# Agent attention with a mixture of experts: the second batch's expert is asked for twelve half steps later in SyncE's order

## The chip, the core and the metric

The kernel runs on one core of a Trainium2 chip. The metric is the device time of one execution in microseconds (us). Engines are named as in the profile: PE is TensorE's matmuls, PEld its weight loads, DVE is VectorE, ACT is ScalarE, POOL is GpSimd and SP is SyncE, which here does no arithmetic but asks for nearly all DMA transfers.

## The reference

Two stages follow each other. Agent attention works on q, k and v of shape [4, 11456, 128] with 49 agents per batch. Its result, 45,824 rows of 128, goes through a mixture of 8 experts with one expert per row.

```python
a2k = softmax(scale * agents @ k^T)        # 49 x 11456, per batch
agent_v = a2k @ v                          # 49 x 128
x = softmax(scale * q @ agents^T) @ agent_v
logits = (x / |x|) @ (emb / |emb|)^T / tau
e = argmax(logits); gate = softmax(logits)[e]
out = gate * (relu(x @ w1[e]) @ w2[e])     # w1: 128 x 1024, w2: 1024 x 128
```

## The kernel before, in words

**Batches.** The four batches are worked through one after another. A batch's rows lie in 23 tiles t (four columns of 128 rows each, the last one smaller), and in 12 units u of two tiles for everything that is loaded. For a batch the kernel first reads all k (scores against the agents, with a running maximum) and all v (`k2_unit`, whose product `avp` is added up in `avx`), folds them in `av_chain` into the agents' values, and then guesses in `pick_expert` the one expert `e0i` that the rows of the batch will want. Rows that turn out to want another expert, or to need more hidden units than were kept, are answered at the end.

**The expert's chain.** `pick_expert` computes `e0i` on PE and DVE (L638 to L647), calls `load_expert`, and then prepares the expert: `total` over the squares of `w1s` (L688 on ACT, L252 on PE), `first_layer` (`gp`, L682), a ranking of the 1024 hidden units by strength (L712 to L755, much of it on DVE), the kept units' matrices `gh` and `gl` (L769, L771), the linear remainder `lin` (L797), the second layer's `w2p` (L810) and `vm` (L832). A tile of the batch starts with `hp` (L1168, L1169), which needs `gh` and `gl`, and goes on with `yp` (L1192 to L1206), which needs `lin` and `w2p`.

**SyncE's queue.** `load_expert` reads the expert's number into a register of SP (L837, which waits for DVE's `e0i`), and then asks for the two matrices `w1s` and `w2s` (L840, L841, 512 KB each). SP works in order, and in the order in which the program was written (`manual_schedule`): loads of k, v and q (`unit_load`, L161) and the transposes through the DMA (`kT`, L481, which needs `ks`; `tt`, L894, which needs POOL's `e`) stand behind whatever stands ahead. The units' tiles `kt`, `vt` and `qt` share one ring of ten buffers (LB), so a load waits until the tile asked for ten loads earlier has been read.

**The order of the program.** Every part is a Python generator. A loop over 92 ticks per batch (23 tiles times 4) runs all of them forward by two half steps a tick, counted in `now`; a `yield n` in `pick_expert` of a batch after the first means "go on n half steps later", since it is spawned with half=True. The order of PE, DVE, ACT and POOL is then made by a planner, which takes a time line of its own and the order of the program as priority. SP keeps the program's order.

**The place of the change in that order.** The counter follows from the program alone. In the kernel before it stands at 220 when the second batch's `load_expert` is reached. The requests on SP that follow are: q unit 11 of the first batch and `kT` of k unit 2 of the third batch at 224, k unit 4 of the third at 226, q unit 0 of the second and `tt` of q unit 9 of the first at 228, k unit 5 of the third at 230 and q unit 1 of the second at 232. The first batch's tile 16 begins its `hp` at 227. `w2p` of the second batch is written at 268, its first tile begins `hp` at 285 and `yp` at 295. The third batch's `load_expert` stands at 394, its `w2p` at 442, its first `yp` at 479.

Of the kernel before, what the change touches and what calls it, by code (L numbers as in the profile page):

```python
# [29 lines left out]
def kernel(ctx: ExitStack, tc: tile.TileContext, q, k, v, agents, emb, tau, w1, w2, out):  # L30
# [517 lines left out]
    def av_chain(b, g):  # L548
# [18 lines left out]
        if b == 0:  # L567
            bt.pick = pick_expert(b, 0)
            next(bt.pick)
        else:  # L570
            spawn(pick_expert(b, 1), 1, half=True)
# [56 lines left out]
    def pick_expert(b, g):  # L628
# [18 lines left out]
        dve.tensor_scalar(e0i, e0i, E - 1, None, ALU.bitwise_and)  # L647
        NM, FV = NMS[b], FVS[b]
        FM = NM * P
        w1s, w2s = load_expert(e0i)  # L650
        bt.e0i = e0i
        bt.e0 = sm.tile([P, 1], F32, name="e0", tag="e0")
# [4 lines left out]
        NX = max(NMS)  # L657
        gh = wk.tile([P, NX * P], F16, name="gh", tag="gh")[:, :FM]
        gl = wk.tile([P, NX * P], F16, name="gl", tag="gl")[:, :FM]
        vm = wk.tile([P, FW], F16, name="vm", tag="vm")[:, :FV]  # L660
# [12 lines left out]
        def col(nm, dt=F32):  # L673
            return sm.tile([P, NF], dt, name=nm, tag=nm)
# [79 lines left out]
        for c in range(NF):  # L754
            dve.tensor_scalar(sel[:, c, :FM], iotaf[:, :FM], rank[:, c : c + 1], None, ALU.is_equal)  # L755
            if c % 4 == 3:
                yield g

        def placed(h, w):
            t_ = psx("placed")[:, :w]  # L760
            with in_place(y_last):
                for c in range(NF):
                    pe.matmul(out=t_, lhsT=gt16[:, h, c].rearrange("p h a -> p (h a)"), rhs=sel[:, c, :w],
                              start=(c == 0), stop=(c == NF - 1))
            return t_

        gmx = sm.tile([P, 2], F32, name="gmx", tag="gmx")
        yield 2 * g
        act.copy(gh, placed(0, FM))  # L769
        yield g  # L770
        dve.tensor_copy(gl, placed(1, FM))  # L771
        bt.gh, bt.gl = gh, gl
# [4 lines left out]
        mask = col("mask")  # L777
        dve.tensor_scalar(mask, rank, FM + FV - 0.5, BIG, ALU.is_lt, ALU.mult)
        yield 1
# [56 lines left out]
    def load_expert(ei):  # L836
        ev = sp.value_load(ei[:1, :1], min_val=0, max_val=E - 1)  # L837
        w1s = ld.tile([P, F], F32, name="w1s", tag="w1s", bufs=1)
        w2s = ld.tile([P, NF, D], F32, name="w2s", tag="w2s", bufs=1)
        sp.dma_start(out=w1s, in_=w1[bass.ds(ev, 1), :, :].rearrange("o d f -> (o d) f"))  # L840
        sp.dma_start(out=w2s, in_=w2[bass.ds(ev, 1), :, :].rearrange("o (c p) d -> p (o c) d", p=P))  # L841
        return w1s, w2s
# [760 lines left out]
    with tc.manual_schedule(engines={mybir.EngineType.SP}):  # L1603
        due = []
        for i in range(len(ticks) + LAG):
            if i < len(ticks):
                b, t, r = ticks[i]
# [12 lines left out]
            while due and due[0][0] <= i:  # L1620
                _, b, t, f = due.pop(0)
# [55 lines left out]
```

## Time and profile before

| | |
|---|---|
| time, median of 3 runs | 741.65 us (741.39 to 742.32) |
| the profiled execution's own time | 741.78 us |
| its span, first to last instruction | 740.0 us |
| PE busy | 688.6 us, 93% |
| DVE, ACT, POOL busy | 77%, 64%, 46% |
| mean granted clock of PE | 0.972 |
| chain that ended last: PE, DVE, DMA, ACT, issue, POOL | 56, 23, 6, 5, 4, 4% |

Busy time and granted clock are read together: a matmul at half clock counts as busy for about twice as long. A bracket behind a row of a time line gives the idle time just before it on its engine and what ended it.

### The profile page before, as it was taken

What the parts mean: (1) busy time and instruction counts of PE and PEld (TensorE: products, weight loads), DVE (VectorE), ACT (ScalarE), POOL (GpSimd) and SP (SyncE); (2) the same over time, 40 slices, a digit from 0 to 9 for tenths busy, and PEclk for the clock granted to TensorE, in tenths of its full rate; (3) what the DMA queues carried; (4) which work ended last, traced back from release to release, by engine and by line L of the source; (5) the groups of instructions that cost most, each with busy time, mean ns of one, the idle gap of its engine ahead of it and who ended that gap; (6) DMA issues with size and microseconds to landing.
All of it is one profiled execution on the core that took longest, in us unless ns stands there. A gap on an engine that the chain in (4) does not pass through costs nothing.

```text
span 740.0 us, 23507 instructions
## 1 busy us (share of the span) xinstructions
PE 688.6 (93%) x9416; PEld 574.9 (78%) x9416; DVE 568.1 (77%) x1499; ACT 475.6 (64%) x1161; POOL 338.8 (46%) x576
## 2 busy tenths in 40 slices
PE   8997889989978899999999889989999999999996
PEld 6886678867867788788888778878897776787675
DVE  4676887864457999988558998965658899789886
ACT  3436858667457757877758837865669447766772
POOL 5003401572245557655615836565638356255410
PEclk9998999999969999999999999999999999999998
DMA  8986239846389786598659439945452247223211
GB/s 329 278 306 215 94 73 249 187 137 197 95 205 342 154 199 166 148 279 214 160 158 268 112 67 253 287 124 159 135 172 94 81 87 194 62 60 115 61 45 64
DMA packets 157817, 122.59 MB, mean 166 GB/s; under 512 B 78727, under 2 KB 134105, under 8 KB 157707
## 3 DMA queue, kind: packets, MB, share of 16 engines
q1 hardware_dynamic: 144331, 97.44, 51.1%
q10 hardware_dynamic: 13120, 23.47, 9.1%
q8 instruction: 74, 1.21, 0.7%
q14 instruction: 36, 0.29, 0.1%
q0 software_dynamic: 256, 0.17, 0.1%
HBM read 79.14 MB, written 23.72 MB: 139 GB/s over the span
## 4 chain that ended last, share of the span: by engine, by line
PE 56%; DVE 23%; DMA 6%; ACT 5%; issue 4%; POOL 4%; SPq 0%; ACTq 0%; POOLq 0%; DVEq 0%
PE sp L430 8%; PE fTp L417 6%; PE avp L521 6%; PE hp L1168 4%; PE hp L1169 4%; PE yp L1192 3%; PE yp L1201 3%; DVE hh L1178 3%; PE yp L1204 3%; PE yp L1206 3%; PE yp L1205 3%; PE vp L1017 3%; DMA kt<-in_k_dram 2%; DVE ot L1220 2%; DMA xq<-in_q_dram,ix 1%
## 5 line engine op out<-in xcount | busy, mean ns | idle before, releaser
L1026 ACT ACTIVATE vp<-vp 128x512 f32<-128x512 f32 x191 | 112.3, 588 | 31.7 <-PE vp L1014 16.3
L1178 DVE SCALAR_TENSOR_TENSOR hh<-hp,hh 128x512 f16<-128x512 f32 (+1 forms) x147 | 98.4, 675 | 24.5 <-ACT hh L1177 23.9
L1204 PE MATMUL yp<-w2p,hh 128*128 128x128 f16 (+1 forms) x582 | 109.9, 220 | 0.0
L1205 PE MATMUL yp<-w2p,hh 128*128 128x128 f16 (+1 forms) x582 | 109.8, 220 | 0.0
L1206 PE MATMUL yp<-w2p,hh 128*128 128x128 f16 (+1 forms) x582 | 108.5, 220 | 0.0
L1177 ACT ACTIVATE hh<-hp 128x512 f16<-128x512 f32 (+1 forms) x147 | 85.1, 587 | 34.9 <-PE hp L1169 28.7
L430 PEld LDWEIGHTS sp<-aT_all,fT 128*64 128x64 f32 (+1 forms) x2400 | 83.7, 140 | 23.2 <-issue 11.5
L430 PE MATMUL sp<-aT_all,fT 128*64 128x49 f32 (+1 forms) x2400 | 97.6, 228 | 3.8 <-DVE qe L874 1.4
L1168 PE MATMUL hp<-tt,gh 128*128 128x512 f16 (+1 forms) x207 | 77.5, 377 | 4.3 <-DVE fT L420 2.4
L1169 PE MATMUL hp<-tt,gl 128*128 128x512 f16 (+1 forms) x207 | 77.8, 378 | 0.0
L965 POOL TENSOR_TENSOR nrm<-qq,half 128x16 f32<-128x16 f32 (+2 forms) x28 | 70.4, 2515 | 0.3
L884 POOL TENSOR_TENSOR e<-qe,e 128x392 f16<-128x392 f32 (+1 forms) x44 | 38.1, 866 | 68.0 <-ACT e L881 67.8
L1220 DVE TENSOR_TENSOR ot<-yp,gs 128x512 f32<-128x512 f32 (+1 forms) x92 | 61.1, 670 | 9.3 <-PE yp L1206 3.7
L1201 PE MATMUL yp<-w2f,hh 128*128 128x128 f32 (+1 forms) x456 | 66.7, 284 | 0.0
L1192 PE MATMUL yp<-lin,tt 128*128 128x128 f16 x720 | 63.3, 221 | 2.9 <-DVE w2p L810 1.4
L1204 PEld LDWEIGHTS <-hh 128*128 128x128 f16 (+1 forms) x582 | 57.6, 99 | 10.3 <-issue 0.5
L422 ACT COPY fT<-fTp 128x512 f32<-128x512 f32 (+1 forms) x87 | 48.6, 563 | 24.7 <-PE fTp L417 17.9
L1206 PEld LDWEIGHTS <-hh 128*128 128x128 f16 (+1 forms) x582 | 57.5, 99 | 8.1 <-issue 1.5
L1205 PEld LDWEIGHTS <-hh 128*128 128x128 f16 (+1 forms) x582 | 57.4, 99 | 5.8 <-issue 0.3
L1201 PEld LDWEIGHTS yp<-w2f,hh 128*128 128x128 f32 (+1 forms) x456 | 58.9, 194 | 2.9 <-issue 1.1
L926 POOL TENSOR_TENSOR rt<-rt 128x384 f32<-128x384 f32 (+1 forms) x48 | 40.5, 843 | 45.1 <-DVE rt L923 42.0
L417 PE MATMUL fTp<-ident,qt 128*128 128x128 f32 x360 | 57.0, 288 | 3.3 <-ACT fT L422 1.1
(373 smaller groups left out, 1786.3 us busy)
## 6 DMA issues: line engine op xcount, KB each, us to landing
kt<-in_k_dram SPq DMA_DIRECT2D x44, 512.0 KB, 6.6
vt<-in_v_dram SPq DMA_DIRECT2D x44, 512.0 KB, 6.2
qt<-in_q_dram SPq DMA_DIRECT2D x44, 512.0 KB, 5.5
out_dram<-ot ACTq DMA_DIRECT2D x88, 256.0 KB, 3.4
w1s<-in_moe_w_dram SPq DMA_DIRECT2D x8, 512.0 KB, 4.6
w2s<-in_moe_w_dram SPq DMA_DIRECT2D x8, 512.0 KB, 5.6
tt<-e SPq DMA_TRANSPOSE x44, 4.1
kt<-in_k_dram SPq DMA_DIRECT2D x4, 96.0 KB, 5.8
```

Source lines behind the costliest of these rows:

```text
L417: pe.transpose(out=tp[:, c * p : (c + 1) * p], in_=src[:p, c0 + c, :], identity=ident[:p, :p])
L430: pe.matmul(out=s[h : h + w, c * A : (c + 1) * A], lhsT=xT[:, c * p + h : c * p + h + w], rhs=aT_all[:, b, :], start=True, stop=True, skip ...
L1026: act.activation(z[:p], z[:p], AF.Relu, scale=-1.0, accum_out=bt.vsum[:p, at : at + 1])
L1168: pe.matmul(out=hp[:, :m], lhsT=bt.gh[:, fs], rhs=tt, start=True, stop=False)
L1169: pe.matmul(out=hp[:, :m], lhsT=bt.gl[:, fs], rhs=tt, start=False, stop=True)
L1177: h_last[:] = [act.activation(hh[:, :m], hp[:, :m], AF.Relu)]
L1178: dve.scalar_tensor_tensor(out=hl[:, :m], in0=hp[:, :m], scalar=0.0, in1=hh[:, :m], op0=ALU.max, op1=ALU.subtract)
L1192: pe.matmul(out=yp[:p, c, :], lhsT=tc_, rhs=bt.lin[:, h], start=(c == 0 and h == 0), stop=False, skip_group_check=True)
L1201: y_last[:] = [pe.matmul(out=y, lhsT=hh[:, cs], rhs=bt.w2f[:, f], start=False, stop=last, skip_group_check=True)]
L1204: pe.matmul(out=y, lhsT=hh[:, cs], rhs=wh, start=False, stop=False, skip_group_check=True)
L1205: pe.matmul(out=y, lhsT=hh[:, cs], rhs=wl, start=False, stop=False, skip_group_check=True)
L1206: y_last[:] = [pe.matmul(out=y, lhsT=hl[:, cs], rhs=wh, start=False, stop=last, skip_group_check=True)]
```

## The change

One statement is added to `pick_expert`. For the second batch alone (b == 1) the generator pauses for twelve half steps after `e0i` was computed and before `load_expert` is called. The read of the number and the two loads are so written into SP's order twelve half steps later, at 232 instead of 220, and everything that `pick_expert` writes behind them moves by the same twelve. Neither an instruction nor a byte is added or taken away.

```diff
         dve.tensor_scalar(e0i, e0i, E - 1, None, ALU.bitwise_and)
         NM, FV = NMS[b], FVS[b]
         FM = NM * P
+        if b == 1:
+            yield 12
         w1s, w2s = load_expert(e0i)
         bt.e0i = e0i
         bt.e0 = sm.tile([P, 1], F32, name="e0", tag="e0")
```

## Rows read from the trace of the kernel before

**Rows 1.** The page's first part: busy us, share of the span, instructions.
```profile
PE 688.6 (93%) x9416; PEld 574.9 (78%) x9416; DVE 568.1 (77%) x1499; ACT 475.6 (64%) x1161; POOL 338.8 (46%) x576
```

**Rows 2.** Waits of SP's queue, 186 to 240: us in total, times, longest.
```profile
SPq L837 <- DVE e0i L647: 16.4, 1, 16.4
```

**Rows 3.** Time line of SP: start us, us, queue, line, what; 186 to 392.
```profile
189.16 0.38 SPq L161 DMA_DIRECT2D kt<-in_k_dram  x1
206.79 0.36 SPq L840 DMA_DIRECT2D w1s<-in_moe_w_dram  x1
...
207.82 0.52 SPq L161 DMA_DIRECT2D qt<-in_q_dram  x1
208.51 4.07 SPq L481 DMA_TRANSPOSE kT<-ks  x1
...
213.77 1.23 SPq L894 DMA_TRANSPOSE tt<-e  x1
...
215.78 0.52 SPq L161 DMA_DIRECT2D qt<-in_q_dram  x1
...
388.12 0.36 SPq L840 DMA_DIRECT2D w1s<-in_moe_w_dram  x1
```

**Rows 4.** Busy time by stretch: stretch, us, engines' busy us, PEclk, DMA share, GB/s.
```profile
202.00:207.00 5.00, 3.17 (x49) 2.81 (x49) 3.07 (x17) 0.96 (x5) 0.97 (x3) 0.99 0.00 0
209.00:213.00 4.00, 1.29 (x19) 1.04 (x18) 0.94 (x4) 2.47 (x5) 3.50 (x3) 0.83 1.08 277
213.00:224.00 11.00, 10.93 (x56) 9.74 (x57) 6.74 (x23) 7.51 (x14) 1.62 (x6) 0.53 1.13 295
226.00:232.00 6.00, 3.54 (x52) 2.73 (x51) 4.96 (x12) 3.81 (x8) 2.33 (x3) 1.00 1.12 335
```

**Rows 5.** Time line of PE, 204 to 229: four of its rows.
```profile
204.37 0.38 PE L252 MATMUL total<-avsq,ones 128*128 128x1 f32 x2 [1.46 <-ACT lr L574]
...
211.53 0.38 PE L252 MATMUL total<-wsq,ones 128*128 128x1 f32 x2 [1.69 <-ACT sel L688]
212.93 0.30 PE L417 MATMUL fTp<-ident,qt 96*128 96x96 f32 x1 [1.02 <-DMA qt<-in_q_dram]
...
227.70 1.09 PE L417 MATMUL fTp<-ident,qt 128*128 128x128 f32 x8 [1.12 <-ACT fT L422]
```

**Rows 6.** Time line of ACT: two rows that waited for a load.
```profile
210.33 1.06 ACT L688 ACTIVATE sel<-w1s 128x1024 f16<-128x1024 f32 x1 [2.69 <-DMA w1s<-in_moe_w_dram]
...
225.86 1.06 ACT L466 ACTIVATE ks<-kt 128x1024 f16<-128x1024 f32 x1 [1.88 <-DMA kt<-in_k_dram]
```

**Rows 7.** Time lines of DVE, POOL and PE: what the seven requests wait for.
```profile
190.99 1.28 DVE L476 SCALAR_TENSOR_TENSOR ks<-kt,hsc,ks 128x1024 f16<-128x1024 f32 x1 [0.35 <-ACT ks L470]
...
198.64 0.91 POOL L884 TENSOR_TENSOR e<-qe,e 128x392 f16<-128x392 f32 x1 [10.20 <-ACT e L881]
...
196.05 1.07 PE L521 MATMUL avp<-vt,kd 128*64 128x129 f32 x16
199.67 1.32 PE L521 MATMUL avp<-vt,kd 128*64 128x129 f32 x20
...
205.79 0.15 DVE L647 TENSOR_SCALAR e0i<-e0i 128x1 int32<-128x1 int32 x1
```

**Rows 8.** Tile w2p, batches 2 and 3: durations ns min/median/max, first and last start.
```profile
L1204 PE MATMUL yp<-w2p,hh x83: 216/219/220, 281.4 to 343.0; 128*128 128x128 f16 x83
L810 DVE CAST w2p<-w2pp x1: 677/677/677, 269.4 to 269.4; 128x512 f16<-128x512 f32 x1
...
L1204 PE MATMUL yp<-w2p,hh x40: 218/219/220, 441.3 to 469.6; 128*128 128x128 f16 x40
L810 DVE CAST w2p<-w2pp x1: 676/676/676, 440.0 to 440.0; 128x512 f16<-128x512 f32 x1
```

**Rows 9.** Busy time by stretch, as rows 4: the chains' later stages.
```profile
235.00:282.00 47.00, 43.92 (x604) 37.30 (x604) 40.92 (x102) 33.03 (x83) 28.85 (x52) 1.00 0.78 198
360.00:400.00 40.00, 39.99 (x530) 35.93 (x528) 22.86 (x63) 25.77 (x63) 14.72 (x21) 1.00 0.65 188
405.00:435.00 30.00, 24.21 (x240) 19.97 (x239) 28.22 (x86) 21.88 (x51) 20.21 (x36) 0.95 0.41 113
432.00:436.00 4.00, 4.00 (x20) 3.58 (x20) 3.97 (x14) 2.80 (x5) 1.42 (x2) 0.57 0.00 0
```

## The prediction

> **What bounds the kernel now.** I read the page's first part, then the clock and the busy time by stretch, then SP's waits, then the time lines around the longest of them. PE is busy for 93% of the span [rows 1], so whatever leaves it idle or at half clock is on the path, and little else is. The stage of the change is one of the few where this happens. SP's longest wait there is the read of the second batch's number: 16.4 us, from 189.5 (end of the k load) to 206 [rows 2, 3]. Behind it the queue is stopped: from 202 to 207 the DMA moves nothing [rows 4]. Then everything comes at once. `w1s` goes out at 206.79, and its square on ACT waits 2.69 us for it [rows 3, 6]; PE, which works in its planned order, waits for that square 1.69 us and then for the q load that stood behind the matrices 1.02 us [rows 5]. From 209 to 213 PE is busy for 1.29 of 4 us, and from 213 to 224 it is busy but at a granted clock of 0.53, so at 1.2 GHz for most of it [rows 4].
>
> **The change, part by part.** Nothing is added; two things move.
>
> First, SP's order. Seven requests (the loop's counter in the section on the kernel names them) now stand ahead of the read: four loads whose buffers must be free, one `kT`, one `tt`, and a last q load. Before, they took from 207.82 to 216.30, 8.5 us, waits among them included [rows 3] (the first and the last of the seven). Were they ready earlier? `ks` for the `kT` is written at 192.27, `e` for the `tt` at 199.55 [rows 7]. The ring of ten gives the first q load the buffer of the third last unit of v, read until 197.12, and the last q load that of the last unit, read until 200.99 (the two `avp` rows) [rows 7]. So they can start at 197.1 and need 8.5 us: SP reaches the read at about 205.6, while `e0i` is written at 205.94 [rows 7]. The read then waits for almost nothing and `w1s` goes out at the same 206.8. If the `kT` takes longer than its 4.07 us the matrices come later by that much; the bound is the whole 8.5 us, should none of the seven start before the read does today. What lies behind the read on SP is as before, but starts at 207.8 where it started at 216.4: 8.6 us earlier. Below, the cost is nothing.
>
> Second, the chain's order. `total`, `first_layer` and all behind them have their priority twelve half steps later. How long is that? The first `yp` of the second and third batch start at 281.4 and 441.3 [rows 8], so 92 ticks or 184 half steps take 159.9 us: 0.87 us a half step, 10.4 us for twelve. So some 10 us of work of the first batch's tiles, which begin at count 227, go ahead of `total`. They need `tt` of unit 8 (transposed before the long wait) and later that of unit 9, which now comes at about 202. `w1s` lands at about 210.3 as before, or up to 3.5 us later if the new loads share the DMA with it (its whole trip was 206.79 to 210.33) [rows 3, 6]; with 10 us of cover PE doesn't see it. If that cover were missing, the 1.69 us would stay.
>
> The terms on PE:
> - the idle time from 209 to 213: 4.00 − 1.29 = 2.7 us goes [rows 4], since both its releasers, the square of `w1s` and the q load, are no longer last.
> - the half clock from 213 to 224: 10.93 us busy at 0.53 is 10.93 × 0.47 = 5.1 us of lost work [rows 4]. Bounds: 5.1 and nothing; I take it whole, because this fall follows the idle stretch of the first term.
> - 226 to 232: 2.46 us idle [rows 4]. The 1.12 us in it go back to ACT, which stood 1.88 us waiting for a k load from the burst [rows 5, 6]; with k loads 8.6 us earlier I count these 1.1 as gone and leave the rest. Bounds: 0 and 2.5.
>
> Together 8.9 us (0 to 10.3). The 1.46 us of waiting at 204 [rows 5] and the thin stretch around it stay: this is `av_chain` itself, which nothing here moves.
>
> On the clock, the trace shows a fall just behind each of these idle stretches. The Trainium skill (TensorE: Matmul & The Clock Gate, "HAM oscillation — how this bites in real kernels") says that every wait for a transfer between bursts of matmuls can send the clock to half again, each time to be paid anew. By that the second fall belongs to the second wait and the 5.1 us go, as I took it; but it also speaks against the change, since a new wait further on would cost its own fall.
>
> **What is given back.** The chain is long. From the asking for `w1s` to `w2p` it took 269.4 + 0.7 − 206.8 = 63.3 us in the second batch and 440.0 + 0.7 − 388.1 = 52.6 us in the third [rows 3, 8]. The third is the model of what comes: there PE was full before and while the matrices came (39.99 of 40 us [rows 9]), and stood later, in the ranking, where DVE was busy for 28.22 of 30 us: from 405 to 435 PE lost 30 − 24.21 = 5.8 us, and a fall of the clock cost 4.00 × 0.43 = 1.7 more: 7.5 us [rows 9]. The second batch lost only 47 − 43.92 = 3.1 us in its ranking, 235 to 282 [rows 9]. If the second becomes like the third, 7.5 − 3.1 = 4.4 us come back. Bounds: 0, since PE now has other work to put there, and 4.4 or more; I take 4.
>
> Sum: −8.9 + 4.0 = −4.9 us. On the profiled execution's 741.78 (its span of 740.0 and 1.8 around it) that is 736.9; it lies 0.1 above the median of the runs, so I say 736.8. From 282 on, the order is the same and I expect the gain to be carried to the end, since PE stays the bound.
>
> **The rivals.**
> - *All of it is won, nothing comes back.* 8.9 to 10.3 us: 731.4 to 732.8. For it: `w2p` was written 11.3 us before its first use (270.1 to 281.4) [rows 8], so even 10.4 us later it would be in time. Against it: that use itself comes 8.9 us earlier.
> - *The gap only moves.* The planner puts no tile between `av_chain` and `total`, or the half clock stays because the idle stretch at 203 alone causes it, or the matrices are 8.5 us late. The second term goes and the first is eaten by the ranking: within 1.5 us of 741.7. For it: the 203 stretch remains, and the clock was already at half for part of 207 to 213 (0.83 over 209 to 213 [rows 4]).
> - *Slower: the chain ends too late for the second batch.* The chain moves by the whole 10.4 us, `w2p` from 270.1 to 280.5, and meets a DVE that is already busy for 40.92 of 47 us [rows 9]. In the third batch `w2p` came 0.6 us ahead of its use. So this decides from the point where `w2p` is written later than about 280.8. If the chain's 63.3 us stretch by a tenth besides, it ends at 286.8 and the first `yp` comes at 287.4, 6 us later than today; half of that PE can fill with the proofs and with the keys of the third batch. 3 us slower: 744.7, up to 748. For it: after the change only 63 half steps (232 to 295) lie between the read and the first `yp`, where the third batch has 85. Against it: the first batch's last tiles run meanwhile without waits.
>
> A rival that the change doesn't do what it says I leave out: the counter is written by the program alone.
>
> **How the numbers follow.** Forecast (4.9 us gained, 733 to 740): 0.50. All won (731.4 to 733): 0.12. The gap only moves (740.2 to 743.1): 0.15. Slower (743.2 to 748): 0.23. A change of under 0.2%, 1.5 us, can't be told from none here; so faster 0.62, same 0.15, slower 0.23. The range leaves out the lowest few hundredths of the second case and about half of the slower one: 732 to 745; the likeliest case's own range is 733 to 740.
>
> **What the changed profile would show.** Right: SP's wait at L837 for `e0i` in this stage falls from 16.4 us to some 5 or less; the DMA is not empty from 197 to 206; `w1s` is still asked for at about 207; between the key of `av_chain` and `total` over `w1s` PE has `hp` and `yp` of the first batch, and no idle stretch of 2 us; the half clock of 213 to 224 is gone or shrinks to some 3 us; the first `yp` from `w2p` of the second batch comes at about 276. Wrong: `w1s` asked for at 211 or later (a request ahead of it was not ready), the clock still at half for 10 us after 207 (then the second term fails), or `w2p` written within 1 us of its first use with PE idle ahead of it and that use later than 281 (the slower rival). If the first `yp` of the second batch comes early but the end does not, the gain was given back in a later batch, which I count as unlikely.

## The result, and the profile after

The kernel after takes 752.07 us (median of 4 runs, 750.05 to 754.0); the kernel before, run beside it, 741.52 (740.43 to 742.32). The ratio is 1.0143, 95% interval [1.0107, 1.0179]: 10.6 us slower where I had forecast 4.9 faster. The profiled execution of after took 754.0 us, with a span of 752.2 against 740.0, 12.2 us more.

The page's first part of after, as [rows 1]: the same instructions and nearly the same busy time, so 11.1 of the 12.2 us are idle time of PE (752.2 − 689.7 = 62.5 us against 740.0 − 688.6 = 51.4).

```profile
PE 689.7 (92%) x9416; PEld 574.1 (76%) x9416; DVE 568.7 (76%) x1499; ACT 476.8 (63%) x1161; POOL 341.8 (45%) x576
```

**What came as forecast.** SP's waits from 186 to 240, against the 16.4 us of [rows 2]:

```profile
SPq L839 <- DVE e0i L647: 4.6, 1, 4.6
```

SP's time line, columns as [rows 3]; the lines of after are two higher than before from L650 on. The seven requests now go out from 189.92 to 203.21, ahead of the read, and the last is done at 203.64. `w1s` is asked for at 209.04, 0.83 us after `e0i` was written at 208.06 + 0.15 (DVE, further down). Before it was 0.85 us. But `e0i` itself comes 2.27 us later than before (205.79): some 1.0 us of that went to the `hp` below and two `fTp`, which ran ahead of the fold that leads to it.

```profile
189.92 0.38 SPq L161 DMA_DIRECT2D qt<-in_q_dram  x1
194.29 1.89 SPq L481 DMA_TRANSPOSE kT<-ks  x1
...
201.10 1.45 SPq L896 DMA_TRANSPOSE tt<-e  x1
202.59 0.58 SPq L161 DMA_DIRECT2D kt<-in_k_dram  x1
203.21 0.43 SPq L161 DMA_DIRECT2D qt<-in_q_dram  x1
209.04 0.36 SPq L842 DMA_DIRECT2D w1s<-in_moe_w_dram  x1
```

**What did not.** PE's time line from 203 to 237, to be held against [rows 5]:

```profile
203.62 0.38 PE L1170 MATMUL hp<-tt,gh 128*128 128x512 f16 x1
...
204.57 0.35 PE L556 MATMUL foldp<-fold,avx 128*128 128x49 f32 x2
...
206.64 0.38 PE L252 MATMUL total<-avsq,ones 128*128 128x1 f32 x2 [1.50 <-ACT lr L574]
206.88 0.37 PE L640 MATMUL key<-enT,sav 128*128 128x8 f32 x2
207.27 0.19 PE L907 MATMUL rtp<-r_hi,tt 128*128 128x58 f16 x1
...
208.77 4.33 PE L430 MATMUL sp<-aT_all,fT 128*64 128x49 f32 x72 [0.35 <-DVE rt L925]
223.93 1.01 PE L1194 MATMUL yp<-lin,tt 128*128 128x128 f16 x8 [10.82 <-DVE ot L1222]
...
231.48 0.28 PE L252 MATMUL total<-wsq,ones 128*128 128x1 f32 x2
```

In the kernel before, PE had this between `total` (211.53) and the same `yp`, which then had nothing to wait for (`gp` ran at half clock; in after, at full clock, the same 16 take 1.97 us):

```profile
213.07 0.38 PE L1168 MATMUL hp<-tt,gh 128*128 128x512 f16 x1
...
214.27 3.54 PE L682 MATMUL gp<-avT,w1s 128*128 128x49 f32 x16
...
219.25 1.03 PE L1192 MATMUL yp<-lin,tt 128*128 128x128 f16 x8
```

Two things are to be seen. The `hp` of the first batch's next tile already ran at 203.62, ahead of the fold (`foldp`), and after the `sp` PE's next instruction is a `yp` that stands 10.82 us; and `total` over `wsq` runs at 231.48, 20.0 us later than in [rows 5]. Its data was there long before: the square of `w1s` starts on ACT at 212.68 and takes 1.06 us.

```profile
212.68 1.06 ACT L690 ACTIVATE sel<-w1s 128x1024 f16<-128x1024 f32 x1 [1.60 <-DMA w1s<-in_moe_w_dram]
...
217.58 1.06 ACT L466 ACTIVATE ks<-kt 128x1024 f16<-128x1024 f32 x1 [1.88 <-DMA kt<-in_k_dram]
...
220.25 0.29 ACT L981 ACTIVATE ex<-lga 128x128 f32<-128x128 f32 x1
```

So from 213.7 on `total` could have run on a PE that did nothing, but it stood behind `yp` in PE's order. `yp` waited for one of its two PSUM buffers, which `ot` empties, and `ot` multiplies by the gate of its rows. The gate's chain begins with the `rtp` at 207.27 (`rt`, `qq`, `nrm`, `cc`, `ex`, `gs`). A k load from the burst held it up on two engines: ACT's `ks` waited for that load, on DVE the gate's `cc`, whose own input (POOL's `nrm`) was there at 216.2, stood behind the `hsc` that needs this `ks`, and on ACT its `ex` stood behind the `ks` too. DVE's rows, with `e0i` for the read above:

```profile
208.06 0.15 DVE L647 TENSOR_SCALAR e0i<-e0i 128x1 int32<-128x1 int32 x1
208.15 0.57 DVE L925 TENSOR_TENSOR rt<-rtp,qe 128x392 f32<-128x392 f32 x1
...
218.76 0.15 DVE L242 TENSOR_SCALAR hsc<-ksq 128x1 int32<-128x1 int32 x1 [3.38 <-ACT ks L466]
...
219.02 0.24 DVE L976 RECIPROCAL cc<-nrm 128x16 f32<-128x16 f32 x1
...
222.55 0.25 DVE L991 RECIPROCAL gs<-el 128x16 f32<-128x16 f32 x1 [0.69 <-POOL el L988]
223.18 1.29 DVE L1222 TENSOR_TENSOR ot<-yp,gs 128x512 f32<-128x512 f32 x2 [0.38 <-ACT gs L995]
```

The stretch in windows, as [rows 4]. The half clock that was to go is still there, now partly over an empty PE:

```profile
205.00:210.00 5.00, 3.13 (x50) 2.78 (x49) 3.82 (x20) 1.46 (x6) 1.70 (x4) 0.87 0.42 169
213.00:224.00 11.00, 0.17 (x4) 0.17 (x3) 4.10 (x12) 5.30 (x12) 3.73 (x8) 0.61 1.13 297
224.00:231.00 7.00, 7.00 (x76) 6.93 (x76) 2.39 (x4) 1.39 (x3) 0.00 (x0) 0.63 1.07 357
```

Tile `w2p` of the second batch, then of the third, as [rows 8]. `w2p` comes 16.3 us later (285.7 against 269.4), the first `yp` that uses it 5.7 us later, and of the 11.3 us in hand 287.1 − 286.4 = 0.7 are left. The third batch's first `yp` is 12.6 us late, about what the span is:

```profile
L1206 PE MATMUL yp<-w2p,hh x77: 217/219/220, 287.1 to 349.8; 128*128 128x128 f16 x77
...
L812 DVE CAST w2p<-w2pp x1: 685/685/685, 285.7 to 285.7; 128x512 f16<-128x512 f32 x1
...
L1206 PE MATMUL yp<-w2p,hh x25: 218/219/220, 453.9 to 473.0; 128*128 128x128 f16 x25
...
L812 DVE CAST w2p<-w2pp x1: 687/687/687, 452.6 to 452.6; 128x512 f16<-128x512 f32 x1
```

**Where the time went.** Windows from `e0i` to the second batch's first `hp` (first row), and then in three steps to the third batch's first `hp`; before:

```profile
205.79:278.40 72.61, 63.94 (x800) 55.73 (x801) 57.62 (x149) 48.18 (x111) 38.94 (x65) 0.91 0.91 234
278.40:319.90 41.50, 40.17 (x651) 33.85 (x650) 39.54 (x109) 32.09 (x89) 28.04 (x49) 1.00 0.60 164
319.90:383.70 63.80, 63.80 (x941) 55.54 (x939) 43.44 (x110) 44.28 (x110) 30.66 (x47) 1.00 0.80 210
383.70:432.20 48.50, 42.44 (x526) 36.48 (x525) 41.55 (x122) 36.47 (x84) 29.45 (x49) 1.00 0.62 162
```

and after:

```profile
208.06:284.50 76.44, 58.95 (x791) 51.85 (x792) 54.24 (x137) 45.70 (x105) 42.91 (x69) 0.87 0.72 185
284.50:327.80 43.30, 41.85 (x653) 35.04 (x654) 39.70 (x107) 30.57 (x84) 22.72 (x40) 1.00 0.48 132
327.80:396.60 68.80, 66.21 (x940) 55.93 (x941) 45.71 (x120) 45.59 (x113) 34.43 (x50) 1.00 0.76 208
396.60:445.50 48.90, 42.70 (x533) 36.83 (x530) 41.23 (x120) 37.00 (x87) 29.42 (x48) 1.00 0.60 160
```

In the first stretch PE's idle time grows from 72.61 − 63.94 = 8.67 to 76.44 − 58.95 = 17.49 us, 8.8 more. The half clock, stretch times what is missing to full clock, comes to 76.44 × 0.13 = 9.9 us against 72.61 × 0.09 = 6.5. But this product also counts the clock over a PE that does nothing: 11.00 × 0.39 = 4.3 of the 9.9 us lie in the window 213 to 224 above, which is idle time already. Where PE works, the half clock took no more than before. The stretch is only 3.8 us longer: it holds 5.0 us less of PE's busy time. These come back in the second batch's tiles, where the busy time rises from 146.41 to 150.76 us (the sums of the last three rows) and the idle time by 2.8. The account doesn't close to the microsecond: the stage ahead of it has 2.9 us less idle time and a mean clock lower by 0.02 over some 206 us, and the rounding of such a mean is worth 2 us there.

The first stretch split at 235, before the ranking (before's part behind 235 is in [rows 9]); first the kernel before up to 235, then after in two rows:

```profile
205.79:235.00 29.21, 23.62 (x256) 21.17 (x257) 20.30 (x55) 17.70 (x36) 12.73 (x17) 0.77 1.04 272
208.06:235.00 26.94, 15.76 (x203) 14.73 (x205) 11.81 (x32) 8.97 (x21) 9.81 (x16) 0.68 0.97 280
235.00:284.50 49.50, 43.19 (x596) 37.12 (x593) 42.43 (x105) 36.73 (x85) 33.10 (x53) 0.97 0.59 134
```

Up to 235 the idle time doubles, from 5.59 to 11.18 us, while the half clock of a working PE falls from some 6.7 (29.21 × 0.23) to 26.94 × 0.32 − 4.3 = 4.3 us: together some 3 us more lost. Behind 235 it is 6.31 us of idle time and 49.50 × 0.03 = 1.5 of half clock, against 3.1 and nothing before: 4.7 us more lost. In the profile of the same kernel run again (e13 below) the wait ahead of `yp` was 8.50 us, and the two parts by the same reckoning are about 1 and 5.5 us.

The ranking shares in the loss. PE's two longest waits from 224 to 285 lie there, behind a DVE busy for 4.92 to 5.00 us of each 5 from 255 to 270:

```profile
260.34 0.59 PE L1019 MATMUL vp<-vm,tt 128*128 128x256 f16 x2 [3.59 <-DVE fT L420]
...
266.27 0.74 PE L765 MATMUL placed<-sel,gt 128*128 128x256 f16 x4 [1.53 <-DVE qe L876]
```

### The profile page after: what moved, and what is told of

Read it like the earlier page. It is cut to its first block, busy times and chain, and to the rows that moved or that the text cites. A ratio compares the mean times of both kernels' runs of the same rounds, so it can differ in the third digit from the quotient of the medians.

```text
span 752.2 us, 23502 instructions
## 1 busy us (share of the span) xinstructions
PE 689.7 (92%) x9416; PEld 574.1 (76%) x9416; DVE 568.7 (76%) x1499; ACT 476.8 (63%) x1161; POOL 341.8 (45%) x576
## 4 chain that ended last, share of the span: by engine, by line
PE 48%; DVE 26%; DMA 9%; ACT 6%; issue 5%; POOL 4%; SPq 0%; ACTq 0%; POOLq 0%; DVEq 0%
PE sp L430 7%; PE fTp L417 7%; PE avp L521 4%; DVE hh L1180 4%; PE yp L1194 3%; DMA kt<-in_k_dram 3%; PE yp L1203 3%; PE hp L1170 3%; PE hp L1171 3%; DVE ot L1222 2%; DMA xq<-in_q_dram,ix 2%; PE yp L1206 2%; PE yp L1207 2%; PE yp L1208 2%; PE vp L1019 2%
## 5 line engine op out<-in xcount | busy, mean ns | idle before, releaser
L1028 ACT ACTIVATE vp<-vp 128x512 f32<-128x512 f32 x191 | 112.4, 588 | 34.3 <-PE vp L1016 16.3
L1222 DVE TENSOR_TENSOR ot<-yp,gs 128x512 f32<-128x512 f32 (+1 forms) x92 | 61.1, 670 | 13.1 <-DMA out_dram<-ot 5.6
L1194 PEld LDWEIGHTS <-tt 128*128 128x128 f16 x720 | 48.9, 99 | 20.5 <-issue 14.3
L1019 PE MATMUL vp<-vm,tt 128*128 128x256 f16 x270 | 53.2, 276 | 8.1 <-DVE fT L420 3.6
```

The source lines that it names most:

```text
L1028: act.activation(z[:p], z[:p], AF.Relu, scale=-1.0, accum_out=bt.vsum[:p, at : at + 1])
L1194: pe.matmul(out=yp[:p, c, :], lhsT=tc_, rhs=bt.lin[:, h], start=(c == 0 and h == 0), stop=False, skip_group_check=True)
L1222: dve.tensor_tensor(out=o[:p, :n], in0=yp[:p, :n], in1=gate, op=ALU.mult)
```

## Experiments

Three causes were in question: the **late chain** (all that stands in `pick_expert` behind the load ends later, and PE runs out of other work first), the **gap** (the 10.8 us ahead of `yp` cost by themselves), and **SP's order** (the load asked for behind seven other requests). Each kernel was timed against the kernel before on its own chip; ratios carry their 95% intervals. "Chain" is the time from `e0i` to `w2p` of the second batch in the profile, both by their start (for e16 it is from an execution some 8 us longer than the median, and by so much uncertain).

| kernel | chain, us | first `yp` from `w2p` | median, us | ratio to before |
|---|---|---|---|---|
| before | 63.6 | 281.4 | 741.5 | 1 |
| after (change, 12) | 77.6 | 287.1 | 752.07 | 1.0143 [1.0107, 1.0179] |
| the same again (e13) | 75.5 | 284.1 | 750.34 | 1.0160 [1.0120, 1.0200] |
| load alone (e1) | 61.3 | 280.5 | 745.57 | 1.0033 [0.9990, 1.0076] |
| load alone again (e15) | 61.3 | 282.1 | 743.18 | 1.0035 [1.0009, 1.0062] |
| chain alone, 12 (e2) | 76.8 | 290.5 | 747.64 | 1.0062 [1.0033, 1.0091] |
| chain alone again (e14) | 76.7 | 284.6 | 745.21 | 1.0083 [1.0054, 1.0112] |
| chain alone, 24 (e16) | 92.7 | 302.1 | 756.80 | 1.0217 [1.0181, 1.0252] |
| change with 6 (e4) | 70.2 | 282.3 | 750.02 | 1.0098 [1.0067, 1.0130] |
| change with 24 (e11) | 89.4 | 295.2 | 757.95 | 1.0197 [1.0144, 1.0250] |
| change, `ks` later (e3) | 76.8 | 283.4 | 752.99 | 1.0146 [1.0083, 1.0210] |
| change, gate early (e5) | 73.8 | 294.1 | 755.31 | 1.0173 [1.0132, 1.0214] |
| before, gate early (e6) | 58.8 | 279.4 | 743.20 | 1.0008 [0.9976, 1.0039] |
| load alone, gate early (e7) | 58.7 | 281.2 | 744.19 | 1.0045 [1.0012, 1.0077] |
| before, chain 10 sooner (e8) | 53.5 | 287.6 | 741.76 | 1.0003 [0.9978, 1.0027] |
| change, chain ranked first (e9) | 72.2 | 282.5 | 747.06 | 1.0068 [1.0035, 1.0102] |
| before, chain ranked first (e10) | 64.8 | 281.9 | 747.04 | 1.0056 [1.0023, 1.0089] |
| third batch instead (e12) | 63.6 | 278.9 | 753.76 | 1.0161 [1.0101, 1.0220] |

**The two halves.** The load alone pauses for ten half steps ahead of the load and drops the pause of ten behind it, so that the chain keeps its place (six of the seven requests go ahead of the read, the last q load does not); the chain alone lengthens that second pause.

```diff
+        if b == 1:
+            yield 10
         w1s, w2s = load_expert(e0i)
...
-        yield 7 + 3 * g
+        if b != 1:
+            yield 7 + 3 * g
```

> SyncE's order alone: the second batch's load_expert ten half steps later (six of the seven requests go ahead of the read), and the pause of ten that follows it in pick_expert left out, so the expert's chain keeps its place in the program. Theory A (the loss comes from the chain being written twelve half steps later: PE has neither total nor gp to put between av_chain and the yp that waits for its gate, and w2p and vm come some 15 us later): about the time before or a little better, 737 to 743, first yp of the second batch with w2p at 277 to 283. Theory B (the loss comes from the order on SyncE: earlier loads, and the squares of k unit 6 of the third batch put ahead of the gate's exponential on ACT): 748 to 753, with PE idle for some 10 us around 213 to 224 as in the changed kernel.

```diff
         w1s, w2s = load_expert(e0i)
...
-        yield 7 + 3 * g
+        yield 7 + 3 * g + (12 if b == 1 else 0)
```

> The chain alone: load_expert at its old place on SyncE, and the pause behind it lengthened by twelve half steps, so that total, first_layer and all behind them are written as late as in the changed kernel. Theory A: 748 to 753, w2p of the second batch at 283 or later and SyncE's wait for the number back at 16 us. Theory B: 740 to 744, since SyncE's order is that of before.

Neither made the whole loss, and the time of the chain alone lay below the change's though its `w2p` came as late. Both were run once more, beside the change, and the chain alone with 24.

> The change itself once more, beside its two halves on one chip. Both theories: 750 to 754 us, 1.2 to 1.7% over before.

> The chain alone 12 half steps later, the load in its old place. Theory A' (the late chain makes the whole loss): within 0.4% of the change, so 748 to 753 us. Rival C' (the load on SP has a share of its own): 745 to 747, at least 0.6% below the change.

> The load alone 10 half steps later, the chain in its old place. Theory A': within 0.3% of before, 740 to 744 us. Rival C': 745 to 748.

> The chain alone 24 half steps later, the load in its old place. Theory A': as much as the change with 24, so 1.7 to 2.2% over before, 754 to 759 us, with `w2p` at some 293. Rival C': about twice the chain alone's 0.62%, 749 to 752.

The load alone costs 0.33 and 0.35%: about 2.5 us, and not the gain of the forecast (the interval of the first run includes no loss, that of the second just doesn't). Its `total` runs at 212.03 behind a wait of 1.75 us (before 1.69), and the wait for the gate then stands ahead of `yp`, 4.90 us. The chain alone costs 0.62 and 0.83%, with 24 half steps 2.17%. In microseconds the first runs fitted no range: 745.57 for the load alone lies between A and B, and 747.64 for the chain alone just under A's; of the second, 743.18 lies in A' and 745.21 in C'. So at 12 the strict form of the late-chain theory (the chain makes everything) falls: the chain alone lies below the change in both pairs, with intervals that do not overlap. The two halves add up to 0.95 and 1.18%, the change cost 1.43 and 1.60; the difference of 0.4 to 0.5% lies within the intervals of these sums. At 24 the chain alone costs as much as the change with 24 (2.17 against 1.97%, intervals that overlap), and the load adds nothing that can be seen.

Where the load's share lies, the traces show. In both profiles of the load alone the stretch from `e0i` to the second batch's first `hp` is 0.4 us shorter than before; the loss stands in the second batch's tiles, the third row of the tables above, which took 63.80 us before. The same stretch in the load alone (e1), the change again (e13) and the chain alone (e14):

```profile
318.50:386.20 67.70, 66.03 (x938) 57.11 (x936) 42.71 (x108) 44.03 (x111) 32.11 (x46) 0.97 0.75 199
```

```profile
324.80:392.80 68.00, 66.26 (x942) 55.98 (x942) 45.74 (x120) 45.65 (x113) 34.50 (x50) 1.00 0.77 211
```

```profile
322.80:388.10 65.30, 64.93 (x934) 55.53 (x932) 44.15 (x115) 43.89 (x110) 31.86 (x46) 1.00 0.74 206
```

It is 3.9 us longer with the load alone (3.8 in e15) and 5.0 and 4.2 with the change (68.80 and 68.00), but only 1.8 and 1.5 with the chain alone (e2, e14). PE's idle time in it is 1.7 us in e1 and 1.7 to 2.6 with the change, but 0.4 in e14. Why a load in another place at 207 costs time after 318 isn't shown.

The window of the load alone (e1) from `e0i` to the second batch's first `hp`, and then that of the chain alone (e14). PE's idle time in them is 9.6 and 13.1 us, the half clock, that over an idle PE included, 72.20 × 0.14 = 10.1 and 76.30 × 0.18 = 13.7 us. This sum is no measure of the loss: for the chain alone it is 26.8 us against 15.2 before, 11.6 more, and the kernel lost 4.7.

```profile
205.90:278.10 72.20, 62.56 (x795) 55.12 (x796) 54.42 (x143) 45.20 (x105) 39.16 (x66) 0.86 0.80 200
```

```profile
203.00:279.30 76.30, 63.23 (x795) 54.09 (x795) 58.51 (x144) 49.28 (x112) 43.93 (x69) 0.82 0.84 221
```

**The dose.** The change's `yield 12` as 6 and as 24.

```diff
         if b == 1:
-            yield 12
+            yield 6
```

> Half the pause: six half steps in place of twelve, so load_expert at 226 and the chain six later. Theory A: the lateness of the chain counts, so about half the loss, 745 to 748. Theory B: the order on ACT and SyncE is what counts, a matter of all or nothing: 741 to 743 or 750 to 753.

> The pause twice as long, 24 half steps instead of 12. Theory A: the cover behind the number has been used up, so each further half step costs nearly its 0.87 us: `w2p` at some 295, 10 us more than the change, 758 to 763 us. Rival B (the stretch ahead of the first batch's `yp` costs by itself): that stretch stands with the gate's data and does not grow, so 751 to 754. Rival D (the time follows SP's order, by which the requests ahead are now served): no more than the change, 748 to 752.

6, 12 and 24 half steps cost 0.98, 1.43 and 1.97%: more with a longer pause, but less for each half step, and the intervals of neighbours overlap. With 6 the time (750.02) lies above the 745 to 748 of theory A and just inside the upper range of B, so this run alone doesn't decide; with 24 (757.95) it lies at the lower edge of A's 758 to 763 and outside the ranges of B and D. Under the gap theory the last step should have cost nothing, since the gap ahead of `yp` was only 4.26 us with 24. The chain alone shows the growth clear of its intervals: 0.62 and 0.83% with 12, 2.17% with 24. The window of the change with 24, as those above: 16.2 us idle, 77.10 × 0.21 = 16.2 us of half clock, that over an idle PE included.

```profile
204.20:281.30 77.10, 60.91 (x767) 52.06 (x767) 52.17 (x135) 45.62 (x105) 45.32 (x71) 0.79 0.67 178
```

**The gap.** First `ks` of one k unit six half steps later, so that ACT serves the gate ahead of it; then the product `rtp` for the gate of one q unit eight half steps sooner (e5, and alone on before and on the load alone).

```diff
+        if (b, u) == (2, 6):
+            yield 6
         i = yield from take(s_slots)
```

> The changed kernel, with the work on k unit 6 of the third batch (its squares and split on ACT and DVE, and its kT) written six half steps later, so that on ACT the gate's ex and gs come ahead of the squares that wait for the k load. Theory C (the 10.8 us in which PE waits for ot are the wait for that k load, handed on through ACT and DVE to the gate): the idle stretch falls from 10.8 to under 6 us and the whole to 746 to 749. If the stretch is as long without it, or the end is the same 752, the k load is not what PE waits for, or the time is lost again by the late chain (theory A).

```diff
-        yield g[3]
-        tts[b, u] = tt
+        if (b, u) == (0, 8):
+            yield g[3] - 4
+
+            def named():
+                yield 4
+                tts[b, u] = tt
+
+            spawn(named())
+        else:
+            yield g[3]
+            tts[b, u] = tt
```

> The changed kernel with the routing product of the first batch's q unit 8 (rtp, and all that hangs on it up to the gate gs of units 7 and 8) written eight half steps sooner, ahead of the second batch's av_chain; the unit is handed to the tiles at its old place. Theory D (the 10.8 us of PE between av_chain and the first yp are the wait for that gate, through ot, which frees the yp buffer; the chain's total and gp were what filled it before): no stretch over 4 us is left between the fold and the first yp, and the time falls to 744 to 749; what remains over 742 is the chain's lateness (w2p still at 280 or later). If the stretch goes and the time stays at 752, the gap was no cost of its own and the chain's lateness is all. If the stretch stays, D is wrong.

> The kernel before with the same earlier routing product. Theory D: before, total, hp and gp filled the wait for the gate only in part (PE was busy for 1.29 of 4 us from 209 to 213), so 736 to 741. If total and gp had nothing to do with it: 741 to 743.

> SyncE's order alone (load_expert ten half steps later, the chain where it was) and the earlier routing product. Theory D: the two together fill the gap from both sides, 735 to 740, the fastest of the four. Without D: as with SyncE's order alone, 743 to 747.

PE's row with the wait in e3, and in e5:

```profile
216.42 1.01 PE L1196 MATMUL yp<-lin,tt 128*128 128x128 f16 x8 [6.73 <-DVE ot L1224]
```

```profile
207.29 1.01 PE L1203 MATMUL yp<-lin,tt 128*128 128x128 f16 x8 [3.13 <-DVE ot L1231]
...
213.51 0.37 PE L640 MATMUL key<-enT,sav 128*128 128x8 f32 x2
```

The gap went from 10.8 to 6.7 and to 3.1 us, and nothing came back: 1.46 and 1.73%, against the 746 to 749 and 744 to 749 us that were hoped for. On the kernel before and on the load alone the earlier gate gained nothing either (1.0008 and 1.0045, where 736 to 741 and 735 to 740 us were expected). The tests have flaws, though. In e3 another wait of 4.5 us came up in the second batch. In e5 the planner put `yp` and `hp` ahead of `key`, which now runs at 213.51 instead of 206.88, so `e0i` itself comes late and `w2p` at 288.5; in e7 too `e0i` came at 215.3. They show that the gap's length doesn't set the time, not that its share in the loss is nothing: `total` stands behind it.

**The chain the other way.** Sooner on before (the pause of ten left out for b == 1); then ranked first in the planner's list, with the change and without it.

> The kernel before with the second batch's chain written ten half steps sooner behind its load, which stays in place: the opposite of the chain's part of the change. Theory A (the chain's place is what is paid for: twelve half steps later cost 0.6%): 737 to 741. If the chain isn't on the path in the kernel before and only becomes so when late: 741 to 744, w2p of the second batch earlier than 269 without use.

```diff
-            spawn(pick_expert(b, 1), 1, half=True)
+            spawn(urgent(pick_expert(b, 1), 1) if b == 1 else pick_expert(b, 1), 1, half=True)
```

> The change with its late read on SP and its late place in the order, but with the second batch's `pick_expert` ranked ahead of all other work in the planner's list (`urgent`), so that each of its steps is taken as soon as its data is there. Theory A (the chain from the expert's number to `w2p` ends too late, and PE runs out of other work in its ranking): `w2p` comes at some 268 to 275 instead of 285.7, the idle time from the number to the second batch's first tiles falls from 17.5 us to 8 to 11, and the time is 741 to 745 us. Rival B (the stretch of 10.8 us ahead of the first batch's `yp` is the cost by itself): it is filled only so far as the chain's matmuls fill it, some 2 us, so 749 to 752. Rival C (the late place of the seven requests on SP, with the ring of buffers and the DMA shared): 750 to 754, with `w2p` early.

> The kernel before with the same ranking (`urgent`) for the second batch's `pick_expert` and no pause: the control for the run above. Theory A: the chain is on the path only when it is late, and before it is not, so 739 to 743 us, within 0.3% of before. Rival B': the ranking itself is worth something whatever the pause: 735 to 738.

A chain 10.1 us shorter gains nothing on before (1.0003): time in hand is already there, and more of it is worth nothing. Ranking the chain first brings the change down to 747.06, against 747.04 for its control: with this rank the pause costs nothing that these runs can tell. But the rank itself cost 0.56%, so the time of 741 to 745 was missed, as were 268 to 275 for `w2p` (278.2) and, for the control, both ranges expected. Nor did the rank do what was meant: `total` still ran behind `yp`, at 225.49 after a gap of 8.49 us, and the chain was 72.2 us long against the control's 64.8. So in that order neither such a gap nor a chain 7.4 us longer cost time that these runs can tell, and the pair shows the pause harmless only there.

**The third batch.**

```diff
+        if b == 2:
+            yield 12
         w1s, w2s = load_expert(e0i)
```

> The pause of 12 half steps for the third batch in place of the second. The third has 85 half steps between the number and its first `yp`, the second 63; but its `w2p` was written only 0.6 us ahead of its use, against 11.3 us in the second. Theory A1 (what counts is the work that is left for PE between the number and the first `yp`, so the longer stretch in the order protects the third): `w2p` some 10 us later, within 2 us of before, 740 to 744. Theory A2 (what counts is how far ahead of its use `w2p` was written): nothing is in hand, so 749 to 754, as much as the change or more.

1.61%: the theory that the longer stretch in the order (85 half steps) protects the third batch falls; the one that goes by what `w2p` has in hand stands, though not as a price: the second batch, with 11.3 us in hand, lost as much. The matrices were asked for 2.4 us after `e0i` (before: 1.3), but from `e0i` to `w2p` it took 70.9 us instead of 53.2, and the first `yp` came 0.0 us behind `w2p` (456.0 − 455.3 − 0.7). The window of the third batch's ranking, up to its first `hp`, is 10.8 us longer than the last row of before above, 2.5 of them idle time and up to 59.30 × 0.12 = 7.1 half clock:

```profile
381.30:440.60 59.30, 50.75 (x573) 42.42 (x572) 43.91 (x123) 39.37 (x90) 31.00 (x52) 0.88 0.55 137
```

This run moves load and chain together. The request came only 1.1 us later, but in the second batch the load cost some 0.3% with no later request, so a share of SP's order isn't excluded here.

## Why the prediction was wrong

**SP's order: right in its result.** The read's wait fell from 16.4 to 4.6 us, the seven requests were done at 203.64, where I had 205.6, and `w1s` went out as soon after `e0i` as before. The way there was not mine: the first q load went out at 189.92, so its buffer was free long before the 197.1 that I read from the ring of ten, and with their waits the seven took 13.7 us, not 8.5. It was worth nothing by itself: the load alone is 0.34% slower, not faster.

**The step that failed is the second: "some 10 us of work of the first batch's tiles, which begin at count 227, go ahead of `total`".** I counted half steps and took the planner's priority for work that is ready. The tile's `hp` had run already, since the planner put it ahead of the fold. What was left, `yp`, waited for the gate. In the kernel before that wait doesn't show because `total`, `fTp`, `hp` and `gp` stood in it (211.53 to 219.25): the expert's chain was itself the cover of the gate's chain. With it put behind, nothing was ready, and PE's order let `yp` hold up a `total` whose data lay there for 17.7 us (213.7 to 231.48). So 10.4 us of delay in the order became 20.0 at `total` and 16.3 at `w2p`.

**The terms.** Idle from 209 to 213 (−2.7) and half clock from 213 to 224 (−5.1): from 213 to 224 PE now works 0.17 of 11 us at a clock of 0.61, and is at 0.63 until 231. The condition I set for the clock, that the idle stretch ahead of it goes, was not met. 226 to 232 (−1.1): PE is full from 225 on; this came true, and is paid for by the gap ahead of it. Of the 8.9 us that were to be won up to 235 none came: idle time and half clock rose by some 3 us there, about 1 in the second profile. The sentence on the clock (a fall behind each idle stretch) holds for the stretches at 203 and 209 only: behind 226 to 232 the clock stayed at 1.00, from 232 to 235 and in 235 to 282 [rows 9].

**What is given back.** I set +4.0 by the model of the third batch, which has nothing in hand and stands in its ranking. Model and size came out: from 235 to the first `hp` 4.7 us more were lost than before (5.5 in the second profile). So the error of the sum lies not here but in the terms ahead of it, and to a lesser part in the second batch's tiles, where 2.8 us of idle time came that I had not counted.

**The rival that came.** "Slower: the chain ends too late for the second batch" gave the place, the point (`w2p` after 280.8; it was 285.7) and even the use (287.4; measured 287.1). Its price, 3 us, was under a third of the truth. I priced the 6 us by which the first `yp` is late and let proofs and keys fill half. But 5.0 us of PE's work that used to lie under the chain were done only after it: the later start of the batch and the work left over both count. The lateness of the first `yp` is no price by itself: with the chain 10 half steps sooner (e8) that `yp` came 6.2 us later than before, and the time was the same.

**What is shown and what isn't.** That lateness of the chain costs by itself and has the larger share (about half of the loss at 12): the chain alone, twice at 12 and above all at 24, since 0.6 to 0.8% is little more than the rank alone cost (0.56%). The third batch agrees but doesn't part chain from load. That SP's late load costs some 0.3% is likely: two runs, one interval just off zero, and a loss at the same place in both profiles. The rest, 0.4% or so of the change's 1.5, is within the noise of these sums, so it isn't shown that there is such a rest; e9 and e10 say that the price of the pause hangs on the order in which PE takes the chain. PE stands idle in the gap ahead of `yp`, but that this sets the time no experiment shows: shortening it gave nothing back, and with the rank one of 8.49 us cost nothing that can be told. Why the load alone is not a gain stays open: the run that takes the gate early besides (e7) stands at 0.45%, but with `e0i` late.

## What to carry to other kernels

Before moving a chain back in an in-order engine's list, name the instruction that will stand in its place and follow that one's own inputs to the end: a priority moves the order, not the readiness. Here a chain whose result had time in hand gained nothing from being sooner and paid when it was later. Its price could not be read from the lateness of its first use, nor from idle time plus half clock over the chain; count half clock only where the engine works, and look at the stretches behind the first use too. And a long wait on a queue is not worth its length if nobody behind it was late.

## What the runs showed that I had not expected

- Rearrangements from which a gain or no change was expected measured 0.03 to 0.56% over before (e8, e6, e1, e7, e10; of these only e7 and e10 are clear of zero); a forecast of half a per cent from one profile, as mine was (4.9 of 741.8 us is 0.66%), is hardly above that.
- One execution says little about half a per cent here: the profiled span of the change was 752.2 us once and 746.1 us another time, with ratios of 1.0143 and 1.0160.
- A transpose on SP took longer in the burst of loads than ahead of it: the same `kT` took 1.89 us in after and 4.07 us in before [rows 3].
